# Attention and two MoE layers on one core: the scales of q, k and v from ScalarE's sums of squares in all four batches

## The chip, the cores and the metric

One Trainium2 chip, one of its cores. The metric is device time in microseconds (us) of one launch; the kernel before was run three times, and its median is 1267.02 us (1266.43 to 1269.06).

## What is computed

Four batches of attention (8 heads, 576 rows, head size 64), whose softmax is cut off below the row's maximum minus tau, then two MoE layers over the 2304 rows that come out (512 wide, 2048 hidden), the first with a rational activation, the second with a piecewise quadratic one. Cut to what matters here:

```python
scores = matmul(q, k.T) / sqrt(64)
scores = where(scores >= max(scores) - tau, scores, -1e9)
attn = exp(scores - max(scores)); attn /= sum(attn) + 1e-9
x = matmul(attn, v)                    # (4, 8, 576, 64) -> (2304, 512)
x = rational(x @ moe_w_in) @ moe_w_out
out = quadratic(x @ moe2_w_in) @ moe2_w_out
```

## The kernel before, in words

The work is done batch by batch. A batch's attention turns q, k and v (float32) into pairs of float16 numbers (a high part and the rest), and for that each tensor gets a scale, a power of two. q and k are prepared for two heads at a time (`prep_pair`, lines 316 to 356; four pairs a batch), v once a batch (`prep_v`, lines 289 to 314).

In batches 1 to 3 the scale comes from the largest magnitude. VectorE reduces the loaded float32 tile to one number per partition (line 332 for q and k in one instruction, line 300 for v in two: 2048 columns, then 512). TensorE spreads these numbers over the partitions and VectorE takes the maximum over them (`everywhere`, lines 179 to 189); `power` (lines 155 to 162) makes the power of two and its reciprocal in three small VectorE instructions. Then `split` (lines 205 to 218) writes the high part on ScalarE and the rest on VectorE into the tile `qk` or `v16`, and for q and k a DMA transposes `qk` (line 346). In batch 0, which is prepared before anything else, line 328 gives ScalarE the same task in another way: a Square of the tile, scaled by 2^-32, whose sum over the columns falls out as an extra output; its elementwise result goes into `qk` as waste and is overwritten by the split. `root` (lines 164 to 173) then makes the power of two from the sum of squares, also in three small VectorE instructions. Batch 0's v has a path of its own (`first_v`, lines 484 to 507).

The tiles matter: the loaded q and k have one buffer (`rqk`), `qk` has one, `v16` has one, and the loaded v (`rw`) two. `v16` of the next batch is free once the last product of attention weights and v of the batch before it has been read; line 307 (a GpSimd memset) is the first to write it in the kernel before.

The order of the work is not written out by hand engine by engine. The kernel issues 192 steps (8 phases: MoE 1 and MoE 2 of each batch in turn; a phase has 3 blocks of 192 rows by 8 chunks of the hidden size), and each step makes a first product (line 846), an activation on ScalarE, VectorE and GpSimd (`rational`, lines 719 to 741, in MoE 1; `quadratic`, lines 785 to 794, in MoE 2) and, three steps later, a second product (line 860). Attention of batches 1, 2 and 3 is spread over steps 18 to 50, 60 to 100 and 108 to 147, so that it runs beside the MoE of the batch before. Every unit has a priority by its step, and when the program is built a planner puts the instructions of each engine in one order by priority and by when it reckons them ready. On the chip each engine then works through its own order, and waits where an operand or a buffer is not there. First products go to two PSUM banks in turn.

The line that is replaced, and the one that takes its place in batch 0:

```python
if b == 0:
    for x in range(2):
        A.activation(qk[:, x, :, 0:D], raw[:, x], AF.Square, scale=2.0**-32, accum_out=mx[:, x : x + 1])
    f = small(2, f"qkf{b}_{pr}")
    s = root(f"qkr{b}_{pr}", f, everywhere(f"mqke{b}_{pr}", mx, 2), 2.0**96, n=2)
else:
    V.tensor_reduce(mx, raw.rearrange("p x c d -> p x (c d)"), axis=AX.X, op=ALU.max, apply_absolute_value=True)
    f, s = power(f"qk{b}_{pr}", everywhere(f"mqke{b}_{pr}", mx, 2), 2)
```

Of the kernel before, what the change touches and what calls it, by code (L numbers as in the profile page):

```python
# [9 lines left out]
F16 = mybir.dt.float16  # L10
# [3 lines left out]
AF = mybir.ActivationFunctionType  # L14
ALU = mybir.AluOpType
AX = mybir.AxisListType
# [26 lines left out]
def tile_attention_moe_moe2(  # L43
# [18 lines left out]
    V, A, G, T, Q = nc.vector, nc.scalar, nc.gpsimd, nc.tensor, nc.sync  # L62
    B, H, S, D = q.shape
    P = 128
    NP = H // 2
    NT = S // P
# [17 lines left out]
    ap = ctx.enter_context(tc.tile_pool(name="ap", bufs=2))  # L84
# [23 lines left out]
    def small(n, name, keep=False):  # L108
        if keep:
            return cp.tile([P, n], F32, name=name)  # L110
        tag = "".join(x for x in name if x.isalpha() or x == "_").rstrip("_")
        return sp.tile([P, n], F32, name=name, tag=f"s{n}_{tag}", bufs=4 if tag in ("mx", "nt") else 2)
# [42 lines left out]
    def power(name, src, n, keep=False):  # L155


        f, s = small(n, name + "_f", keep), small(n, name + "_s", keep)
        V.tensor_scalar(f, src, 1.0 / TOP, TINY / TOP, op0=ALU.mult, op1=ALU.max)
        V.tensor_scalar(f.bitcast(I32), f.bitcast(I32), 0x7F800000, None, op0=ALU.bitwise_and)  # L160
        V.reciprocal(s, f)
        return f, s

    def root(name, f, src, up, even=False, n=1):


        s = small(n, name + "_s")
        V.tensor_scalar(f.bitcast(I32), src.bitcast(I32), 1, 0x3F000000 if even else 0x3F800000,
                        op0=ALU.logical_shift_right, op1=ALU.bitwise_and)
        top = TOP / 2 if even else TOP  # L170
        V.tensor_scalar(f, f, up / top, (2.0 if even else 1.0) * TINY / top, op0=ALU.mult, op1=ALU.max)
        V.reciprocal(s, f)
        return s
# [5 lines left out]
    def everywhere(name, src, n, keep=False, place=None):  # L179


        r = small(n, name, keep)
        if place is None:
            place = ps_1.tile([P, 512], F32, name="pm" + name, tag="aux")
        pm = place[:, 0 : n * P].rearrange("p (n q) -> p n q", n=n)
        for i in range(n):
            T.matmul(pm[:, i], src[:, i : i + 1].to_broadcast([P, P]), ident, start=True, stop=True)
        V.tensor_reduce(r, pm, axis=AX.X, op=ALU.max)  # L188
        return r
# [15 lines left out]
    def split(hi, lo, src, scale=None, on_vector=True):  # L205

        if scale is None:
            A.copy(hi, src)  # L208

            n = E // 4 if tuple(src.shape) == (P, E) else None  # L210
            for p in [slice(c, c + n) for c in range(0, E, n)] if n else [slice(None)]:
                G.tensor_tensor(lo[:, p], src[:, p], hi[:, p], op=ALU.subtract)  # L212
        elif on_vector:
            A.activation(hi, src, AF.Copy, scale=scale)
            V.scalar_tensor_tensor(lo, src, scale, hi, op0=ALU.mult, op1=ALU.subtract)
        else:
            A.activation(src, src, AF.Copy, scale=scale)
            split(hi, lo, src)
# [63 lines left out]
    f_x, s_x = [None] * B, [None] * B  # L282
# [3 lines left out]
    def whole(x):  # L286
        return x[..., 0 : NT * P, :].rearrange("h (p t) d -> p h (t d)", t=NT)

    def prep_v(b, on_vector=True):

        raws = []
        mx = small(2, f"mv{b}")
        for g in range(2):
            raw = rp.tile([P, H if g else H * NT, D], F32, name=f"rv{b}_{g}", tag="rw")
            if g:
                for i in range(2):
                    Q.dma_start(raw[i * ST : (i + 1) * ST], v[b, :, NT * P :, :].rearrange("h p d -> p h d"))
            else:
                Q.dma_start(raw.rearrange("p (h t) d -> p h (t d)", h=H), whole(v[b]))
            V.tensor_reduce(mx[:, g : g + 1], raw.rearrange("p t d -> p (t d)"), axis=AX.X, op=ALU.max,  # L300
                            apply_absolute_value=True)
            raws.append(raw)
        m1 = small(1, f"mv1{b}")
        V.tensor_reduce(m1, mx, axis=AX.X, op=ALU.max)
        f_x[b], s_x[b] = power(f"v{b}", everywhere(f"mve{b}", m1, 1), 1, True)
        vv = ap.tile([P, H * (NT + 1), 2 * D + 2], F16, name=f"v16_{b}", tag="v16", bufs=1)
        G.memset(vv[:, :, D : D + 1], 1.0)
        for g, raw in enumerate(raws):
            n = H if g else H * NT
            for n0 in range(0, n, 8):  # L310
                n1 = min(n, n0 + 8)
                to = vv[:, g * H * NT + n0 : g * H * NT + n1]
                split(to[:, :, 0:D], to[:, :, D + 1 : 2 * D + 1], raw[:, n0:n1], s_x[b], on_vector)
        return vv

    def prep_pair(b, pr, on_vector=True):
        raws = rp.tile([P, 2, C + 1, D], F32, name=f"rqk{b}_{pr}", tag="rqk", bufs=1)
        raw = raws[:, :, 0:C, :]
        for x, src in enumerate((q, k)):
            Q.dma_start(raws[:, x].rearrange("p (a c) d -> p a (c d)", a=2)[:, :, 0 : NT * D],  # L320
                        whole(src[b, 2 * pr : 2 * pr + 2]))
            for ab in range(2):
                Q.dma_start(raw[ab * ST : (ab + 1) * ST, x, NT, :], src[b, 2 * pr + ab, NT * P :, :])
        mx = small(2, f"mqk{b}_{pr}")
        qk = ap.tile([P, 2, C, 2 * D], F16, name=f"qk{b}_{pr}", tag="qk", bufs=1)
        if b == 0:
            for x in range(2):
                A.activation(qk[:, x, :, 0:D], raw[:, x], AF.Square, scale=2.0**-32, accum_out=mx[:, x : x + 1])
            f = small(2, f"qkf{b}_{pr}")
            s = root(f"qkr{b}_{pr}", f, everywhere(f"mqke{b}_{pr}", mx, 2), 2.0**96, n=2)  # L330
        else:
            V.tensor_reduce(mx, raw.rearrange("p x c d -> p x (c d)"), axis=AX.X, op=ALU.max, apply_absolute_value=True)
            f, s = power(f"qk{b}_{pr}", everywhere(f"mqke{b}_{pr}", mx, 2), 2)

        con = sp.tile([P, 4], F32, name=f"con{b}_{pr}", tag="con", bufs=3)
        V.scalar_tensor_tensor(con[:, 0:1], f[:, 0:1], cflag, f[:, 1:2], op0=ALU.mult, op1=ALU.mult)
        V.tensor_scalar(con[:, 1:2], con[:, 0:1], -1.0, None, op0=ALU.mult)
        V.scalar_tensor_tensor(con[:, 2:3], s[:, 0:1], tau8, s[:, 1:2], op0=ALU.mult, op1=ALU.mult)
        V.tensor_tensor(con[:, 2:3], con[:, 2:3], tlow, op=ALU.min)
        if b == 0:  # L340
            V.tensor_scalar(con[:, 3:4], con[:, 2:3], STEEP, -LARGEST, op0=ALU.mult, op1=ALU.max)
        for x in range(2):
            split(qk[:, x, :, 0:D], qk[:, x, :, D : 2 * D], raw[:, x], s[:, x : x + 1], on_vector)
        if b > 0 or pr < 2:
            qkT = ap.tile([P, 2 * C, P], F16, name=f"qkT{b}_{pr}", tag="qkT")
            Q.dma_start_transpose(out=qkT, in_=qk.rearrange("p x c d -> p (x c d)"))
            qT, kT = qkT[:, 0:C], qkT[:, C : 2 * C]
            kT2 = ap.tile([P, C, P], F16, name=f"kT2{b}_{pr}", tag="kT2")
        else:
            qT, kT, kT2 = (ap.tile([P, C, P], F16, name=f"{x}{b}_{pr}", tag="eT" if pr == 2 else "hl", bufs=N_ROW)  # L350
                           for x in ("qT", "kT", "kT2"))
            for x, t in enumerate((qT, kT)):
                Q.dma_start_transpose(out=t, in_=qk[:, x].rearrange("p c d -> p (c d)"))
        Q.dma_start(kT2[0:D], kT[D : 2 * D])
        Q.dma_start(kT2[D : 2 * D], kT[0:D])
        return con, qT, kT, kT2
# [515 lines left out]
    for n in range(N_FIRST):  # L872
        with at(36 * n / N_FIRST - 40):
            next(att)
        while halves and len(halves) * N_FIRST > 2 * NCH * (N_FIRST - 1 - n):
            with at(2.4 * (2 * NCH - len(halves)) - 40):
                i, x = halves.pop(0)
# [83 lines left out]
```

## Time and profile before

| | |
|---|---|
| Median of three runs | 1267.02 us (1266.43 to 1269.06) |
| The profiled execution's own time | 1266.28 us |
| Its span | 1264.5 us |
| Mean granted TensorE clock | 0.956 |
| TensorE matmul busy | 1096.8 us (87% of the span) |
| VectorE busy | 1003.2 us (79%) |
| ScalarE busy | 824.5 us (65%) |
| GpSimd busy | 534.4 us (42%) |

The span is the part of the execution between its first and last instruction; the time has 1.8 us more around it. A busy share is a mean over the whole span, and the stages of this kernel are limited by different engines, so the stretches have to be read one by one. In rows of the trace PE is TensorE's matmul, PEld its weight load, DVE is VectorE, ACT ScalarE, POOL GpSimd and SP the queue that issues the DMAs; L332 is line 332 of the kernel.

### The profile page before, as it was taken

What the parts mean: (1) busy time and instruction counts of PE and PEld (TensorE: products, weight loads), DVE (VectorE), ACT (ScalarE), POOL (GpSimd) and SP (SyncE); (2) the same over time, 40 slices, a digit from 0 to 9 for tenths busy, and PEclk for the clock granted to TensorE, in tenths of its full rate; (3) what the DMA queues carried; (4) which work ended last, traced back from release to release, by engine and by line L of the source; (5) the groups of instructions that cost most, each with busy time, mean ns of one, the idle gap of its engine ahead of it and who ended that gap; (6) DMA issues with size and microseconds to landing.
All of it is one profiled execution on the core that took longest, in us unless ns stands there. A gap on an engine that the chain in (4) does not pass through costs nothing.

```text
span 1264.5 us, 31682 instructions
## 1 busy us (share of the span) xinstructions
PE 1096.8 (87%) x12618; PEld 985.3 (78%) x12618; DVE 1003.2 (79%) x2371; ACT 824.5 (65%) x1473; POOL 534.4 (42%) x700
## 2 busy tenths in 40 slices
PE   2788778668788998999799999998889998999998
PEld 1454445567788887899688898997778998999997
DVE  7767977899997877789999766899997767897431
ACT  2476767668686677667676666777765766775332
POOL 3324546576553645421355454313454553222221
PEclk9797898779899999999999999999999999999999
DMA  7656657633427545933398548522784469006000
GB/s 206 221 171 213 231 193 248 239 114 98 117 73 234 114 98 100 241 124 84 73 225 193 94 91 205 178 53 58 214 185 76 102 148 243 14 2 237 32 14 26
DMA packets 220341, 176.40 MB, mean 139 GB/s; under 512 B 182048, under 2 KB 193312, under 8 KB 212000
## 3 DMA queue, kind: packets, MB, share of 16 engines
q1 hardware_dynamic: 220192, 174.36, 51.6%
q8 instruction: 99, 1.62, 0.5%
q14 instruction: 50, 0.41, 0.1%
HBM read 106.83 MB, written 21.50 MB: 101 GB/s over the span
## 4 chain that ended last, share of the span: by engine, by line
PE 37%; DVE 32%; DMA 11%; ACT 8%; issue 5%; POOL 5%; SPq 2%; DVEq 0%; ACTq 0%; POOLq 0%
PE ph L846 14%; PE acc L860 14%; DMA eT<-hl 6%; DVE e L387 3%; DVE sc L425 2%; PE pv L596 2%; DVE t L734 2%; DMA qkT<-qk 2%; PE pv L413 2%; DVE t L740 2%; DVE t L729 2%; DVE wt L229 2%; DMA rqk<-in_k_dram 2%; POOL hl L398 1%; DVE t L730 1%
## 5 line engine op out<-in xcount | busy, mean ns | idle before, releaser
L860 PE MATMUL acc<-gg,wc 128*128 128x192 f16 x4608 | 427.6, 247 | 16.7 <-DVE mye L188 8.4
L846 PEld LDWEIGHTS <-wc 128*128 128x128 f16 x4608 | 389.4, 99 | 30.0 <-DVE t L731 14.7
L860 PEld LDWEIGHTS <-wc 128*128 128x128 f16 x4608 | 383.7, 98 | 19.4 <-issue 17.8
L212 POOL TENSOR_TENSOR gg<-t,gg 128x384 f16<-128x384 f32 x192 | 187.6, 978 | 407.0 <-ACT gg L208 332.4
L846 PE MATMUL ph<-xT,wc 128*128 128x192 f16 x2304 | 220.1, 253 | 19.8 <-DVE t L731 15.3
L846 PE MATMUL ph<-yT,wc 128*128 128x192 f16 x2304 | 216.6, 246 | 2.3 <-DVE t L731 1.9
L398 POOL TENSOR_TENSOR hl<-e,hl 128x256 f16<-128x256 f32 x216 | 154.3, 735 | 0.0
L208 ACT CAST gg<-t 128x384 f16<-128x384 f32 x192 | 97.2, 508 | 83.9 <-DVE t L793 39.4
L387 DVE SCALAR_TENSOR_TENSOR e<-sc,nt,e 128x576 f32<-128x576 f32 x108 | 95.7, 886 | 33.0 <-ACT e L386 32.2
L792 DVE SCALAR_TENSOR_TENSOR t<-t,c 128x384 f32<-128x384 f32 x96 | 63.5, 662 | 72.6 <-ACT t L791 72.5
L386 ACT ACTIVATE e<-sc,nt,con 128x576 f32<-128x576 f32 x108 | 93.5, 866 | 7.2 <-POOL hl L398 0.2
L395 ACT CAST hl<-e 128x576 f16<-128x576 f32 x108 | 72.2, 669 | 35.6 <-DVE e L387 34.7
L727 ACT ACTIVATE t<-ph,sc 128x384 f32<-128x384 f32 x96 | 55.2, 575 | 60.8 <-PE ph L846 60.5
L791 ACT ACTIVATE t<-ph,c 128x384 f32<-128x384 f32 x96 | 64.0, 666 | 47.2 <-PE ph L846 46.7
L396 POOL TENSOR_TENSOR hl<-e,hl 128x64 f16<-128x64 f32 x108 | 40.0, 371 | 126.9 <-ACT hl L395 126.5
L413 PE MATMUL pv<-v,eT 128*128 128x65 f16 (+3 forms) x1680 | 70.7, 194 | 25.2 <-DMA eT<-hl 24.9
L425 DVE TENSOR_SCALAR_CACHE_REDUCE sc<-s 128x576 f32<-128x576 f32 x108 | 80.9, 749 | 13.3 <-PE s L380 12.8
L413 PEld LDWEIGHTS <-eT 128*128 128x128 f16 (+1 forms) x1680 | 62.9, 100 | 35.0 <-DMA eT<-hl 32.4
L732 ACT ACTIVATE t<-t,lc 128x384 f32<-128x384 f32 x96 | 67.9, 707 | 20.4 <-DVE t L729 19.8
L734 DVE SCALAR_TENSOR_TENSOR t<-t,ka,t 128x384 f32<-128x384 f32 x96 | 68.4, 713 | 13.9 <-ACT t L733 13.4
L212 POOL TENSOR_TENSOR wh<-wt,wh 128x256 f16<-128x256 f32 x64 | 60.6, 977 | 41.5 <-ACT wh L208 32.1
L212 POOL TENSOR_TENSOR wc<-wt,wc 128x256 f16<-128x256 f32 x64 | 55.4, 897 | 47.1 <-ACT wc L208 47.1
(233 smaller groups left out, 1901.5 us busy)
## 6 DMA issues: line engine op xcount, KB each, us to landing
wc<-scratch SPq DMA_DIRECT2D x56, 1024.0 KB, 5.9
rw<-in_moe_w_in_dram SPq DMA_DIRECT2D x16, 1024.0 KB, 5.9
rw<-in_moe_w_out_dram SPq DMA_DIRECT2D x16, 1024.0 KB, 5.6
scratch<-wc SPq DMA_DIRECT2D x8, 1024.0 KB, 5.8
scratch<-wh SPq DMA_DIRECT2D x16, 512.0 KB, 3.5
rqk<-in_q_dram SPq DMA_DIRECT2D x16, 256.0 KB, 3.0
rqk<-in_k_dram SPq DMA_DIRECT2D x16, 256.0 KB, 3.1
kT<-qkT SPq DMA_DIRECT2D x28, 144.0 KB, 2.4
```

Of the source, the lines that this page charges most:

```text
L208: A.copy(hi, src)
L212: G.tensor_tensor(lo[:, p], src[:, p], hi[:, p], op=ALU.subtract)
L386: A.activation(e, s, AF.Exp, bias=nb, scale=con[:, 0:1])
L387: V.scalar_tensor_tensor(e, s, th, e, op0=ALU.is_ge, op1=ALU.mult)
L395: A.copy(hi, e)
L398: G.tensor_tensor(lo_w[:, p], e[:, whole][:, p], hi[:, whole][:, p], op=ALU.subtract)
L413: T.matmul(pv[rows, 0:w], eT[:, c, cols], vv[:, h * NT + x if x < NT else H * NT + h, at : at + w], start=(n == 0), stop=(n == len(blocks) ...
L425: V.tensor_scalar(s, banks[:, 0:S], 1.0, -LARGEST, op0=ALU.mult, op1=ALU.max, accum_out=mx)
L732: A.activation(r, u, AF.Ln, bias=lc[:, 1:2], scale=lc[:, 0:1])
L734: V.scalar_tensor_tensor(s, s, ka[:, 0:1], r, op0=ALU.add, op1=ALU.mult)
L846: last = T.matmul(ph[:, f, :], w[:, wx, kt, f * P : (f + 1) * P], rhs, start=(n == 0), stop=(n == 3 * KT - 1))
L860: T.matmul(dst, w[:, wx, f, d * P : (d + 1) * P], gg[:, gx, f, :], start=(i == 0 and f == 0 and n == 0 and d % 2 == 0), stop=(i == NCH - 1 ...
```

## The change

In batches 1 to 3 the two kinds of VectorE reduction go away. For each pair of heads ScalarE makes two Squares with a sum over the columns (576 columns each, q then k), as batch 0 has them; for v it makes two (2048 and 512 columns), whose waste goes into `v16`, so that tile is now allotted ahead of the loads. `root` takes the place of `power` for these scales. Batch 0 and `first_v` stay.

```diff
-    def root(name, f, src, up, even=False, n=1):
+    def root(name, f, src, up, even=False, n=1, keep=False):
...
-        s = small(n, name + "_s")
+        s = small(n, name + "_s", keep)
...
         mx = small(2, f"mv{b}")
+        vv = ap.tile([P, H * (NT + 1), 2 * D + 2], F16, name=f"v16_{b}", tag="v16", bufs=1)
         for g in range(2):
...
-            V.tensor_reduce(mx[:, g : g + 1], raw.rearrange("p t d -> p (t d)"), axis=AX.X, op=ALU.max,
-                            apply_absolute_value=True)
+            n0, n1 = (H * NT, H * (NT + 1)) if g else (0, H * NT)
+            A.activation(vv[:, n0:n1, 0:D], raw, AF.Square, scale=2.0**-32, accum_out=mx[:, g : g + 1])
             raws.append(raw)
         m1 = small(1, f"mv1{b}")
         V.tensor_reduce(m1, mx, axis=AX.X, op=ALU.max)
-        f_x[b], s_x[b] = power(f"v{b}", everywhere(f"mve{b}", m1, 1), 1, True)
-        vv = ap.tile([P, H * (NT + 1), 2 * D + 2], F16, name=f"v16_{b}", tag="v16", bufs=1)
+        f_x[b] = small(1, f"v{b}_f", True)
+        s_x[b] = root(f"v{b}", f_x[b], everywhere(f"mve{b}", m1, 1), 2.0**96, keep=True)
         G.memset(vv[:, :, D : D + 1], 1.0)
...
-        if b == 0:
-            for x in range(2):
-                A.activation(qk[:, x, :, 0:D], raw[:, x], AF.Square, scale=2.0**-32, accum_out=mx[:, x : x + 1])
-            f = small(2, f"qkf{b}_{pr}")
-            s = root(f"qkr{b}_{pr}", f, everywhere(f"mqke{b}_{pr}", mx, 2), 2.0**96, n=2)
-        else:
-            V.tensor_reduce(mx, raw.rearrange("p x c d -> p x (c d)"), axis=AX.X, op=ALU.max, apply_absolute_value=True)
-            f, s = power(f"qk{b}_{pr}", everywhere(f"mqke{b}_{pr}", mx, 2), 2)
+        for x in range(2):
+            A.activation(qk[:, x, :, 0:D], raw[:, x], AF.Square, scale=2.0**-32, accum_out=mx[:, x : x + 1])
+        f = small(2, f"qkf{b}_{pr}")
+        s = root(f"qkr{b}_{pr}", f, everywhere(f"mqke{b}_{pr}", mx, 2), 2.0**96, n=2)
```

## Rows read from the trace of the kernel before

**Rows 1.** The page, part 1: busy us, share of the span, instructions.

```profile
PE 1096.8 (87%) x12618; PEld 985.3 (78%) x12618; DVE 1003.2 (79%) x2371; ACT 824.5 (65%) x1473; POOL 534.4 (42%) x700
```

**Rows 2.** The page, part 4: the chain that ended last, shares of the span by engine.

```profile
PE 37%; DVE 32%; DMA 11%; ACT 8%; issue 5%; POOL 5%; SPq 2%; DVEq 0%; ACTq 0%; POOLq 0%
```

**Rows 3.** Windows, three stretches: length, busy us by engine, clock, DMA share, GB/s.

```profile
300.00:350.00 50.00, 36.50 (x374) 34.02 (x372) 49.90 (x126) 36.68 (x68) 25.89 (x31) 0.86 0.38 98
600.00:675.00 75.00, 64.08 (x781) 58.05 (x780) 74.97 (x195) 54.58 (x102) 36.18 (x47) 0.98 0.71 164
875.00:925.00 50.00, 41.32 (x496) 37.54 (x494) 50.00 (x119) 34.92 (x65) 23.50 (x32) 0.97 0.77 201
```

**Rows 4.** Those three stretches summed: L332 alone, then L300 alone.

```profile
sum 175.00, DVE 5.35; mean DVE 1.78
...
sum 175.00, DVE 5.90; mean DVE 1.97
```

**Rows 5.** Windows 250:300, 575:600 and 825:875 summed: all, L332 alone, L300 alone.

```profile
sum 125.00, PE 107.02 PEld 102.91 DVE 120.10 ACT 92.58 POOL 50.65; mean PE 35.67 PEld 34.30 DVE 40.03 ACT 30.86 POOL 16.88
...
sum 125.00, DVE 2.71; mean DVE 0.90
...
sum 125.00, DVE 2.93; mean DVE 0.98
```

**Rows 6.** Windows of the MoE 1 stretch before attention of batches 2 and 3.

```profile
550.00:575.00 25.00, 25.00 (x301) 24.96 (x299) 21.72 (x39) 18.01 (x34) 5.49 (x6) 1.00 0.12 43
800.00:825.00 25.00, 25.00 (x327) 24.78 (x325) 21.98 (x47) 19.41 (x37) 6.94 (x8) 1.00 0.46 147
```

**Rows 7.** Groups by line, VectorE: busy us, mean ns, idle us before, its releaser.

```profile
L332 DVE TENSOR_REDUCE mqk<-rqk 128x2 f32<-128x1152 f32 x12 | 16.2, 1347 | 7.1 <-DMA rqk<-in_k_dram 7.1
...
L300 DVE TENSOR_REDUCE mv<-rv 128x1 f32<-128x2048 f32 (+1 forms) x6 | 8.8, 1472 | 0.0
```

**Rows 8.** Waits in total: us, times, longest us.

```profile
DVE mqk L332 <- DMA rqk<-in_k_dram: 7.1, 6, 1.9
```

**Rows 9.** Groups by line, VectorE: first small instruction of `power` and of `root`.

```profile
L159 DVE TENSOR_SCALAR qk_f<-mqke 128x2 f32<-128x2 f32 x12 | 4.2, 351 | 0.1
L168 DVE TENSOR_SCALAR qkf<-mqke 128x2 int32<-128x2 int32 x4 | 1.1, 282 | 0.1
```

**Rows 10.** Timeline of ScalarE in batch 0: start us, length us, the Squares of L328.

```profile
9.70 0.68 ACT L328 ACTIVATE qk<-rqk 128x576 f16<-128x576 f32 x1 [2.76 <-DMA rqk<-in_q_dram]
10.29 0.19 ACT L328 ACTIVATION_READ_ACCUMULATOR qk<-rqk 128x1 f32 x1
10.46 0.68 ACT L328 ACTIVATE qk<-rqk 128x576 f16<-128x576 f32 x1
```

**Rows 11.** Groups by line, ScalarE: one kind of instruction at 384 and 576 columns.

```profile
L208 ACT CAST gg<-t 128x384 f16<-128x384 f32 x192 | 97.2, 508 | 83.9 <-DVE t L793 39.4 <-DVE t L740 20.7 <-PE acc L860 17.8
...
L395 ACT CAST hl<-e 128x576 f16<-128x576 f32 x108 | 72.2, 669 | 35.6 <-DVE e L387 34.7
```

**Rows 12.** Timelines of VectorE and PE: two reductions, each followed by its reader on PE.

```profile
305.11 1.34 DVE L332 TENSOR_REDUCE mqk<-rqk 128x2 f32<-128x1152 f32 x1
...
306.59 0.68 PE L187 MATMUL pmmqke<-ident,mqk 128*128 128x128 f32 x4 [1.11 <-DVE rm L700]
...
335.30 1.33 DVE L332 TENSOR_REDUCE mqk<-rqk 128x2 f32<-128x1152 f32 x1
...
405.73 0.64 PE L187 MATMUL pmmqke<-ident,mqk 128*128 128x128 f32 x4
```

**Rows 13.** Timelines of VectorE, POOL and PE: batch 2's v.

```profile
325.27 2.27 DVE L300 TENSOR_REDUCE mv<-rv 128x1 f32<-128x2048 f32 x1
...
541.97 0.28 POOL L307 MEMSET v<- 128x40 f16 x1 [4.65 <-PE pv L413]
...
582.27 0.41 PE L187 MATMUL pmmve<-ident,mv 128*128 128x128 f32 x2
```

**Rows 14.** Timeline of ScalarE: the one load of an activation table.

```profile
0.73 1.28 ACT L92 ACT_TABLE_LOAD   x1 [0.73 <-PEq L946]
```

## The prediction, on record before the changed kernel was run

> **What bounds the kernel now.** I read the page's busy shares first: TensorE is busy 87% of the span, VectorE 79%, ScalarE 65% [rows 1]. None is full, so the means decide nothing. The chain of waits comes next: 37% of it is TensorE's, 32% VectorE's, only 8% ScalarE's [rows 2]; two engines take turns. Windows of 25 and 50 us show where. In 300 to 350, 600 to 675 and 875 to 925, where a batch's preparation and first attention rows run beside MoE 1, VectorE is busy 174.9 of 175 us, while TensorE is busy 141.9 and ScalarE 126.2 [rows 3]: there VectorE alone sets the pace, and TensorE has 33 us to spare. In 250 to 300, 575 to 600 and 825 to 875 VectorE is at 120.1 of 125 (96%) with TensorE at 107.0 [rows 5]: nearly so. In MoE 1 ahead of attention, 550 to 575 and 800 to 825, TensorE is busy 25.0 of 25.0 at a granted clock of 1.00, the full 2.4 GHz [rows 6]; time taken from VectorE there buys nothing.
>
> **What is removed.** Twelve reductions of q and k at 1.347 us, 16.2 us, and six of v, 8.8 us: 25.0 us of VectorE [rows 7]. What they are worth depends on where they stand.
> - In the three full stretches stand 5.35 us of line 332 and 5.90 of line 300, 11.25 us [rows 4]. With VectorE never idle its queue gets shorter by just that, and TensorE's 33 us of slack can take it up: worth 11.25.
> - In the three nearly full stretches stand 2.71 and 2.93, 5.64 us [rows 5]. Between nothing and all of it; VectorE's idle 4.9 us there show that other waits intervene, so I take half: 2.8.
> - The other 25.0 - 16.9 = 8.1 us (six reductions of q and k) stand where VectorE has gaps or TensorE is full. I count them at nothing. What hides them is the wait for the load: VectorE idled 7.1 us in front of six of the twelve [rows 8]. If the cover were gone they would be worth 8.1.
> Removed: 14.05 us, at most 25.0. The low bound comes from the readers. A reduction of pair 1 of a batch is read by its matmul within 6 us (three of them, at 305 the matmul follows at once); the others run far ahead, such as that at 335.30, read at 405.73 [rows 12]. If only the three count, 3 x 1.34 = 4.0 us.
>
> **What is added.** Batch 0's Squares give the price. Square and accumulator read follow each other 0.59 and 0.17 us apart, so one costs ScalarE 0.76 us, although the instruction lasts 0.68 [rows 10]. For q and k 24 x 0.76 = 18.2 us. No row has a Square of 2048 columns, so I scale: a cast takes 508 ns at 384 columns and 669 at 576, 0.84 ns a column [rows 11]; 0.76 + 1472 x 0.00084 = 2.00 us for 2048 and 0.76 - 0.05 = 0.71 for 512, 2.7 a batch, 8.1 in all. ScalarE gets 26.3 us, VectorE loses 25.0; as engine time the trade is even. It pays only if ScalarE has room: it is busy 72% of the full stretches [rows 3].
> - Of ScalarE's busy time, 8% of 1264.5 = 101 us lies on the chain, 12% of 824.5 [rows 1, 2]. At that share the Squares cost 3.2 us. From below: nothing, if all fall into gaps. From above: VectorE's own share, 405 of 1003 us or 40%, 10.6 us.
> - The wait for the raw q and k moves with them. VectorE's 7.1 us [rows 8] become ScalarE's, with the Exp, casts and PSUM reads of attention and MoE queued behind in the same order. At 12%: 0.9 us; from above the whole 7.1; from below nothing.
> - `root` for `power` is three small instructions for three. The first takes 282 ns in place of 351 [rows 9]; over 15 uses that is 1.0 us of VectorE at best. Nothing counted; its cover is that both readings hold stray long ones.
> - A new wait: the Squares write `qk` and `v16`, which have one buffer each, where the reductions wrote neither. For q and k the transposing DMA that frees `qk` is issued ahead of the next pair's load on SP, so the load still comes last; SP's own order does not change. For v it matters: batch 2's reduction ran at 325.27, but `v16` came free only near 541.97, when GpSimd's memset was released, and the number is read at 582.27 [rows 13]. The Squares get 40 us for 2.7, enough; batch 3 has the like. So no latency, but these 5.4 us of ScalarE move to stretches where TensorE is full and ScalarE busy 18.0 and 19.4 of 25 [rows 6]; that is inside the 12%. GpSimd's memset may fall in behind a Square: 0.28 us, covered by the same 40.
> - Squares need no other activation table: a single load, at 0.73 us, served batch 0's Squares and every Exp [rows 14].
>
> **The sum,** against the profiled execution's own 1266.28 us (span 1264.5 and 1.8 around it): 1266.28 - 14.05 + 3.2 + 0.9 = 1256.3. That execution is 0.7 below the median of the three runs, so on the median's footing 1257.0, a gain of 10.0 us.
>
> **A rule that speaks against it.** On the trace, one pass over q and k costs VectorE 1.35 us and ScalarE 2 x 0.76 = 1.52 [rows 7, 10]. The Trainium skill, "ScalarE: Activation LUTs", section "Rules for kernel authors", says to give multiplications and maxima to VectorE and not to ScalarE, since VectorE is up to about three times faster per element in bf16. Here, in float32, the rows make ScalarE only 13% dearer for q and k; for v, 2.7 against 2.9, cheaper by the estimate. By that rule the change would lose, which is the second rival below.
>
> **The rivals.**
> - *The removed time was filler.* The planner places early whatever it reckons ready, so a reduction read 70 us later may have cost nobody anything. Then the gain is the 4.0 us of pair 1, the cost 4.1, the time 1267.1. For it: rows 12. Against it: VectorE without a gap in 175 us, filler or not [rows 3].
> - *ScalarE's queue holds up the others.* A Square of 2 us, or one waiting for its load, stands ahead of the instructions that empty PSUM, and TensorE has two banks for first products. Place: the stretches where TensorE is full, and the attention rows. Price: 40% of 26.3 and all the 7.1 of waiting, 17.7 us, against 14.05: 3.6 us slower, 1270.6. It decides once ScalarE's cost passes 14.05 + 2.5. For it: batches 2 and 3's v lands where TensorE is full [rows 6]. Against it: ScalarE holds only 8% of the chain [rows 2]. This is where the skill's rule would lead.
> - *All of it counts.* The whole 25.0 us leave the path and ScalarE costs 4.1: 1246.1. Against it: the six reductions behind a load wait [rows 8].
>
> A planner works on all this anew, so instructions elsewhere may change places too; no row prices that, and it is why the range reaches past the terms' own.
>
> **How the numbers follow.** 0.2%, about 2.5 us, is what a measurement of this kernel can tell from no change. My forecast has 0.52: the gain between 5 and 15 us, 1252 to 1262. The filler case 0.15, the ScalarE queue 0.25, all of it 0.08. Faster is 0.52 + 0.08 = 0.60, same 0.15, slower 0.25. The range takes in the forecast, the filler case and the nearer half of both outer cases: 1247 to 1271.
>
> **What would show it.** Right: VectorE's busy time falls to about 978 us and ScalarE's rises to about 851; the stretches of full VectorE come out shorter by some 11 us in all and TensorE's share in them rises; v's Squares of batches 2 and 3 stand after the last product of the batch before. Wrong: waits of ScalarE for the load of k beyond some 4 us followed by idle TensorE; TensorE waiting for first-product banks in the stretches of rows 6; or VectorE still full over the same 175 us, filled by other work.

## The result and the profile after

The changed kernel takes 1248.24 us (median of four, 1242.5 to 1254.8) beside 1266.72 for the kernel before (four, 1260.6 to 1269.1): ratio 0.9873, interval [0.9836, 0.9909]. (The recorded ratio is not the quotient of the two medians, which is 0.9854.) By the medians it is 18.5 us faster where 10.0 were forecast, by the interval 11.5 to 20.8: inside the range of 1247 to 1271 but near its low end. Executions of one and the same kernel lie up to 17 us apart here, so single traces are read below for where things stand, and medians for what they cost.

The page of the changed kernel, profiled in an execution of 1242.5 us, the fastest of the four: its span, part 1 and part 4 [rows 1, 2].

```profile
span 1240.7 us, 31727 instructions
...
PE 1091.9 (88%) x12618; PEld 984.5 (79%) x12618; DVE 977.1 (79%) x2353; ACT 842.9 (68%) x1533; POOL 543.0 (44%) x700
...
PE 35%; DVE 19%; DMA 9%; ACT 6%; POOL 6%; issue 6%; SPq 1%; DVEq 0%; ACTq 0%; POOLq 0%
```

VectorE lost 26.1 us of busy time. ScalarE gained 18.4, not 26.3. Since the span also shrank by 23.8, VectorE's busy share stayed at 79%. Its part of the chain reads 19% where the chain before had 32%, but that is no result: the shares printed here sum to 82%, those before to 100%, and a second profile of the changed kernel, in the run that times it again below, has 27% with all of the chain printed:

```profile
PE 39%; DVE 27%; DMA 12%; POOL 8%; issue 8%; ACT 6%; SPq 1%; DVEq 0%; ACTq 0%; POOLq 0%
```

The windows that answer to [rows 3], where VectorE is full in the changed kernel, with their sum.

```profile
300.00:325.00 25.00, 17.28 (x176) 15.43 (x174) 25.00 (x67) 20.91 (x43) 13.16 (x17) 0.93 0.29 86
575.00:650.00 75.00, 66.06 (x815) 61.36 (x813) 74.97 (x194) 57.45 (x110) 37.84 (x46) 0.98 0.70 176
825.00:900.00 75.00, 65.82 (x785) 61.45 (x784) 75.00 (x197) 59.00 (x114) 29.38 (x36) 0.98 0.58 140
sum 175.00, PE 149.16 PEld 138.24 DVE 174.97 ACT 137.36 POOL 80.38; mean PE 49.72 PEld 46.08 DVE 58.32 ACT 45.79 POOL 26.79
```

In windows of 25 us VectorE is still full for 175 us. The stretches lie elsewhere: the first has lost its second half, the second comes 25 us earlier, the third 50 us earlier and 25 us longer. TensorE gets 149.2 us of work done in them in place of 141.9. ScalarE is busy 137.4 us there in place of 126.2, and is still not full. Windows this wide cannot show a change of 11 us; with 5 us ones, from 200 to 1000 us, those in which VectorE is busy 4.98 us or more add up to 275 us before and 245 in the changed kernel (255 in its second profile).

The windows that answer to [rows 6], MoE 1 ahead of attention.

```profile
525.00:550.00 25.00, 25.00 (x303) 24.97 (x302) 21.09 (x39) 20.41 (x40) 5.06 (x6) 1.00 0.29 102
775.00:825.00 50.00, 50.00 (x631) 49.56 (x630) 44.76 (x97) 39.81 (x76) 12.07 (x16) 1.00 0.39 104
```

TensorE is as full as before, at a granted clock of 1.00, with three of the four Squares of batches 2's and 3's v now beside it; the fourth starts at 523.10, just ahead of the first window.

The groups of the Squares on ScalarE, all 32 of q and k (8 of them batch 0's) and the six of v, which stand in the place of [rows 7].

```profile
L328 ACT ACTIVATE qk<-rqk 128x576 f16<-128x576 f32 x32 | 21.7, 677 | 26.8 <-DMA rqk<-in_q_dram 15.9 <-DMA rqk<-in_k_dram 5.6 <-DMA qkT<-qk 3.8
...
L302 ACT ACTIVATE v<-rv 128x2048 f16<-128x2048 f32 (+1 forms) x6 | 7.6, 1270 | 1.8 <-DMA rv<-in_v_dram 1.4 <-PE pv L410 0.4
```

And their waits in total [rows 8].

```profile
ACT qk L328 <- DMA rqk<-in_q_dram: 15.9, 4, 9.8
...
ACT qk L328 <- DMA rqk<-in_k_dram: 5.6, 6, 1.6
ACT qk L328 <- DMA qkT<-qk: 3.8, 2, 2.2
...
ACT qk L328 <- issue: 1.4, 1, 1.4
```

Batch 0's eight alone waited 13.5 us of this for q and 2.3 for k (the same view from 0 to 95 us). So the new Squares wait 2.4 + 3.3 us for their loads, where VectorE had waited 7.1, and 3.8 us, in two waits together, for the transposing DMA that frees `qk`.

The timeline of ScalarE at batch 2's v [rows 13] (start, duration, what it is, and the wait ahead of it).

```profile
523.10 1.91 ACT L302 ACTIVATE v<-rv 128x2048 f16<-128x2048 f32 x1 [0.42 <-PE pv L410]
524.92 0.18 ACT L302 ACTIVATION_READ_ACCUMULATOR v<-rv 128x1 f32 x1
525.01 0.61 ACT L302 ACTIVATE v<-rv 128x512 f16<-128x512 f32 x1
```

The same view at a pair of q and k [rows 10].

```profile
399.05 0.68 ACT L328 ACTIVATE qk<-rqk 128x576 f16<-128x576 f32 x1 [1.60 <-DMA qkT<-qk]
399.63 0.19 ACT L328 ACTIVATION_READ_ACCUMULATOR qk<-rqk 128x1 f32 x1
399.73 0.67 ACT L328 ACTIVATE qk<-rqk 128x576 f16<-128x576 f32 x1
```

v's Square starts as soon as the last product of batch 1's attention releases `v16`, as foreseen, and lasts 1.91 us. The pair at 399.05 is the only new one that runs back to back, 0.68 us apart. But whatever ScalarE does next after a new Square of q or k starts 0.66 to 0.69 us after it in 23 of 24 cases, although an accumulator read of 0.19 us stands between: the read hides in the overlap of neighbours.

### The profile page after: what moved, and what is told of

It reads as the page before. It is cut to its first block, busy times and chain, and to the rows that moved or that the text cites. A ratio compares the mean times of both kernels' runs of the same rounds, so it can differ in the third digit from the quotient of the medians.

```text
span 1240.7 us, 31727 instructions
## 1 busy us (share of the span) xinstructions
PE 1091.9 (88%) x12618; PEld 984.5 (79%) x12618; DVE 977.1 (79%) x2353; ACT 842.9 (68%) x1533; POOL 543.0 (44%) x700
## 4 chain that ended last, share of the span: by engine, by line
PE 35%; DVE 19%; DMA 9%; ACT 6%; POOL 6%; issue 6%; SPq 1%; DVEq 0%; ACTq 0%; POOLq 0%
PE ph L843 15%; PE acc L857 15%; DMA eT<-hl 7%; POOL hl L395 3%; DVE e L384 2%; PE pv L410 2%; DVE t L731 2%; DVE t L726 2%; DVE sc L422 2%; DVE t L737 1%; DMA qkT<-qk 1%; DVE t L728 1%; POOL gg L212 1%; DVE t L727 1%; ACT hl L392 1%
## 5 line engine op out<-in xcount | busy, mean ns | idle before, releaser
L843 PEld LDWEIGHTS <-wc 128*128 128x128 f16 x4608 | 389.8, 99 | 37.4 <-issue 20.8
L212 POOL TENSOR_TENSOR gg<-t,gg 128x384 f16<-128x384 f32 x192 | 193.3, 1008 | 380.0 <-ACT gg L208 330.0
L393 POOL TENSOR_TENSOR hl<-e,hl 128x64 f16<-128x64 f32 x108 | 43.3, 401 | 145.0 <-ACT hl L392 141.4
L422 DVE TENSOR_SCALAR_CACHE_REDUCE sc<-s 128x576 f32<-128x576 f32 x108 | 80.9, 749 | 13.5 <-PE s L377 12.7
L731 DVE SCALAR_TENSOR_TENSOR t<-t,ka,t 128x384 f32<-128x384 f32 x96 | 70.1, 730 | 11.1 <-ACT t L730 10.8
```

Of the source, the lines that this page charges most:

```text
L422: V.tensor_scalar(s, banks[:, 0:S], 1.0, -LARGEST, op0=ALU.mult, op1=ALU.max, accum_out=mx)
L731: V.scalar_tensor_tensor(s, s, ka[:, 0:1], r, op0=ALU.add, op1=ALU.mult)
L843: last = T.matmul(ph[:, f, :], w[:, wx, kt, f * P : (f + 1) * P], rhs, start=(n == 0), stop=(n == 3 * KT - 1))
```

## The experiments

The kernel's order of instructions is made by a planner when the program is built. Taking 18 instructions from one engine and giving 30 to another changes the order as well. So there are two theories: **1**, VectorE's time is what counts; **2**, the other order is. Several runs keep the order exactly: the planner sees the full instruction, and its columns are cut or doubled in the finished program.

**Before's order, all 18 reductions short.**

```diff
+            CUT.append(V.tensor_reduce(mx, raw.rearrange("p x c d -> p x (c d)"), axis=AX.X, op=ALU.max, apply_absolute_value=True).ins.name)
...
+    def short(args):
+        return [replace(args[0], ap=[*args[0].ap[:-1], (1, 8)]), *args[1:]]
+    for block in nc.main_func.blocks:
+        for at, ins in enumerate(block.instructions):
+            if ins.name in CUT:
+                block.instructions[at] = replace(ins, ins=short(ins.ins))
```

> The kernel before with its order of instructions on every engine kept exactly, and only the 18 reductions made short once the order is fixed (8 columns for each number in place of 512 to 2048; the scales then come from fewer columns, which is the work left out). VectorE loses about 22 of its 25 us of reductions; ScalarE gets nothing. Theory 1 (VectorE's time in the stretches where it is full is what counts): about 12 us faster than before, near 1254, shorter stretches of full VectorE, nothing gained before 275 us. Theory 2 (the changed kernel gains because the planner made another order): 0 to 4 us faster, 1263 or more.

Measured: 1253.03 us beside 1264.50, ratio 0.9913 [0.9886, 0.9940], 11.5 us faster. The groups of its reductions, and its windows at the times of [rows 3].

```profile
L332 DVE TENSOR_REDUCE mqk<-rqk 128x2 f32<-128x16 f32 x12 | 2.0, 164 | 6.3 <-DMA rqk<-in_k_dram 6.2
...
L300 DVE TENSOR_REDUCE mv<-rv 128x1 f32<-128x8 f32 x6 | 0.9, 153 | 1.5 <-DMA rv<-in_v_dram 1.4
```

```profile
300.00:350.00 50.00, 38.42 (x408) 36.10 (x406) 48.41 (x127) 38.85 (x72) 27.66 (x32) 0.90 0.34 88
600.00:675.00 75.00, 64.56 (x807) 58.86 (x807) 74.23 (x197) 54.86 (x105) 38.27 (x51) 0.98 0.84 192
875.00:925.00 50.00, 44.21 (x570) 39.92 (x569) 49.83 (x124) 36.54 (x69) 27.19 (x37) 1.00 0.80 216
```

22.1 us of VectorE went (25.0 - 2.9), with no other order and nothing given to ScalarE, and 11.5 us of time went with them, 0.52 us for each. At the old times VectorE now has gaps of 1.6, 0.8 and 0.2 us, and TensorE does 147.2 us in place of 141.9. Theory 1 holds for the size.

**The same, only pairs 1 and 2 and v short; and only pairs 0 and 3 short.** In the diff of the first run the condition is added in these two forms:

```diff
+            CUT.extend([...] * (pr in (1, 2)))
...
+            CUT.extend([...] * (pr in (0, 3)))
```

> The order of the kernel before, kept exactly; of the 18 reductions only those that stood in full or nearly full stretches of VectorE are made short (pairs 1 and 2 of each batch, and v: 16.9 us of reductions). Theory 1: these carry the whole gain of the run with all 18 short, so 10 to 13 us below the kernel before. If the place in the trace says nothing: 16.9/25 of that gain, 7 to 8 us.

> The counterpart: only the six reductions of pairs 0 and 3 are made short, 8.1 us that stood where VectorE has gaps or TensorE is full. Theory 1: nothing, within 2 us of the kernel before. If the place says nothing: 3 to 4 us faster.

Measured: 1257.08 beside 1264.04 (0.9952 [0.9932, 0.9973]), 7.0 us faster; and 1261.66 (0.9980 [0.9962, 0.9998]), 2.4 us faster. The first took away 15.0 us of reductions (16.9 became 1.9), the second 7.1 (8.1 became 1.0), so 0.46 and 0.33 us for each. The first run misses what theory 1 expected, 10 to 13 us. These are the numbers expected if the place says nothing. The spans of the two profiled executions say the opposite:

```profile
span 1253.4 us, 31682 instructions
```

```profile
span 1264.4 us, 31682 instructions
```

Beside the 1264.5 of the trace before that is 11.1 and 0.1 us, theory 1 to the letter. But the twelve executions of each kernel spread over 17 and 12 us, and one execution cannot outweigh them. The place of the reductions is not shown to matter as much as the prediction had it; the two parts together, 9.4 us, agree with the first run.

**The changed kernel's order, Squares short (one column in 64), and Squares long.**

```diff
+            CUT.extend([A.activation(...).ins.name] * (b > 0))
...
+                block.instructions[at] = replace(ins, ins=short(ins.ins), outs=short(ins.outs))
```

In the long form only q's and k's Squares change: each group of 64 columns is read twice, so 576 columns become 1152.

```diff
+                block.instructions[at] = replace(ins, ins=long(ins.ins, lambda d: [d[0], (64, 9), (0, 2), (1, 64)]), outs=long(ins.outs, lambda d: [*d[:-1], (1, 128)]))
```

> The changed kernel with its order kept exactly, and the 30 Squares of batches 1 to 3 made short once the order is fixed (one column in 64; the scales come from fewer columns, which is the work left out). ScalarE loses about 18 of the 26 us that the Squares cost it. If ScalarE's time costs 12%, as the prediction has it: 2 to 3 us faster than the changed kernel. If it costs 40% (the second rival): about 7 us faster. If it costs nothing: the same within 2 us.

> The changed kernel with its order kept exactly, and the 24 Squares of q and k in batches 1 to 3 made twice as long once the order is fixed (each reads its 576 columns twice and fills the whole of its part of the tile, which the split overwrites anyway). ScalarE gets about 11.5 us more. At the predicted 12% that is 1 to 2 us slower than the changed kernel; at 40%, the second rival, 4 to 5 us slower.

Measured: 1246.45 for the short ones (0.9859 [0.9821, 0.9897]) and 1249.43 for the long ones (0.9868 [0.9839, 0.9897]). The changed kernel timed again beside the long ones gave 1247.39, its first timing 1248.24. The Squares' groups, short and then long:

```profile
L328 ACT ACTIVATE qk<-rqk 128x9 f16<-128x9 f32 (+1 forms) x32 | 11.1, 347 | 32.0 <-DMA rqk<-in_q_dram 20.0 <-DMA rqk<-in_k_dram 8.8 <-DMA qkT<-qk 2.0
...
L302 ACT ACTIVATE v<-rv 128x32 f16<-128x32 f32 (+1 forms) x6 | 1.5, 289 | 3.1 <-DMA rv<-in_v_dram 1.6 <-PE pv L410 1.5
```

```profile
L328 ACT ACTIVATE qk<-rqk 128x1152 f16<-128x1152 f32 (+1 forms) x32 | 33.2, 1036 | 25.2 <-DMA rqk<-in_q_dram 18.5 <-DMA rqk<-in_k_dram 4.2 <-DMA qkT<-qk 1.4
```

ScalarE's busy time went from 842.9 to 826.3 us in the one and from 843.5 to 853.4 in the other. 16.6 us less brought 1 to 2 us, 9.9 more cost 2. The intervals overlap with the changed kernel's, so each run alone settles little. Set against each other, the two differ by 27.1 us of ScalarE and by 3.0 us of time (by the ratios 1.1), with some 6 us of uncertainty by the two intervals. That excludes 40%, which would be 10.8 us, and fits 12% as well as no price at all. The waits for q's and k's loads do not go when the Squares shrink: 20.0 and 8.8 us with short ones, 15.9 and 5.6 in the changed kernel.

**Squares and reductions together.** The reductions are put back beside the Squares, their result unused, first with one column in 64, then in the same order at full length.

```diff
+            CUT.append(V.tensor_reduce(old, raw[..., 0], axis=AX.X, op=ALU.max, apply_absolute_value=True).ins.name)
```

> The changed kernel with the old reductions put back beside the Squares, their result unused, and made short (one column in 64). The planner makes a new order for it. Theory 1: the time of the changed kernel within the spread that another order brings, so 1242 to 1258. Theory 2 gives no number: any order may come out.

> The same order to the instruction as the run with the short reductions put back, but the 18 reductions have their full length again: VectorE has its 25 us back, ScalarE keeps its 26 us of Squares. Theory 1: 10 to 14 us slower than the run with the short ones. Theory 2: 0 to 4 us slower, since the order is the same.

Measured: 1256.78 (0.9954 [0.9935, 0.9974]) and 1269.24 (1.0041 [1.0027, 1.0054]). The groups of the reductions in the two:

```profile
L334 DVE TENSOR_REDUCE oqk<-rqk 128x2 f32<-128x18 f32 x12 | 2.1, 175 | 8.9 <-DMA rqk<-in_k_dram 8.9
L306 DVE TENSOR_REDUCE ov<-rv 128x1 f32<-128x32 f32 x3 | 0.6, 194 | 0.0
L306 DVE TENSOR_REDUCE ov<-rv 128x1 f32<-128x8 f32 x3 | 0.5, 158 | 0.7 <-DMA rv<-in_v_dram 0.7
```

```profile
L334 DVE TENSOR_REDUCE oqk<-rqk 128x2 f32<-128x1152 f32 x12 | 16.1, 1346 | 8.1 <-DMA rqk<-in_k_dram 8.0
...
L306 DVE TENSOR_REDUCE ov<-rv 128x1 f32<-128x2048 f32 x3 | 6.8, 2276 | 0.0
L306 DVE TENSOR_REDUCE ov<-rv 128x1 f32<-128x512 f32 x3 | 2.0, 673 | 0.0
```

21.7 us of VectorE cost 12.5 us at the same order, 0.57 us for each: the first run's price again, in a third order, with ScalarE's Squares present. With both kinds of work the kernel is in this order slower than the kernel before, so Squares alone do not make it faster. The short form is 9 us slower than the changed kernel, though it adds only 3.2 us of VectorE. It has another order; but with the reductions VectorE's waits for loads came back as well, 8.9 + 0.7 us, and this run does not separate the two.

**The same work in another order.** One number of the priorities is moved, in the kernel before and in the changed one.

```diff
-                with at(t - 1.5):
+                with at(t - 1.4):
                     next(atts[u[1]])
```

> The kernel before with the same work, and only the priority of the attention units moved by a tenth of a step (1.4 in place of 1.5 steps ahead), so that the planner makes another order. Theory 1: within 3 us of before. Theory 2 (orders differ by as much as the change brought): it may lie 5 to 15 us off, either way.

> The changed kernel with the same tenth of a step. Theory 1: it stays 8 to 16 us below the kernel before with the same tenth of a step. Theory 2: the difference between those two may be anything from 0 to 30 us, and this kernel may lie 5 to 15 us off the changed one.

> The kernel before with the priority of the attention units moved a tenth of a step the other way (1.6 steps ahead). The tenth of a step late gave 6 to 8 us more with the same work, so this should differ from before by a like amount, in either direction: 1257 to 1272.

> The changed kernel with the same tenth of a step early. If the work (VectorE's time less ScalarE's cost) is worth about 10 us and an order a few us either way, it lies 5 to 16 us below the kernel before with the same tenth; a difference outside that would say that the order decides more than the work.

> The changed kernel unchanged, timed again beside the kernel before on the chip of the other runs of this call, since its first four executions spread over 12 us. If theory 1 and a good order each gave their part: 13 to 17 us below the kernel before. If the first four were lucky: 9 to 12 us.

| order | kernel before | changed kernel | difference |
|---|---|---|---|
| as it is | 1265.37 | 1247.39 (0.9860 [0.9829, 0.9890]) | -18.0 |
| a tenth of a step late | 1270.78 (1.0061 [1.0032, 1.0089]) | 1256.18 (0.9943 [0.9922, 0.9965]) | -14.6 |
| a tenth early | 1269.10 (1.0037 [1.0019, 1.0054]) | 1259.53 (0.9951 [0.9928, 0.9974]) | -9.6 |

The ratios are to the kernel before, as it is: 1264.50 beside the late pair, 1265.37 in the other rows. With no change of work an order moves the time by 4 to 12 us. Both kernels have the best of their three orders as they are. In each of the three the changed one wins, by 14.1 us in the mean. The changed kernel timed again, 18.0 us below, is past even the 13 to 17 expected of it: its first four executions were not lucky ones.

Where the order shows first: the windows from 0 to 275 us, TensorE's first products alone (busy us and count in brackets), of the kernel before, the kernel before with short reductions, the kernel before replanned late, the changed kernel, its second profile, the changed kernel replanned late, and Squares together with short and with full reductions.

```profile
0.00:275.00 275.00, 18.19 (x153) 0.85 0.64 210
```

```profile
0.00:275.00 275.00, 19.25 (x166) 0.86 0.66 210
```

```profile
0.00:275.00 275.00, 18.46 (x153) 0.85 0.65 210
```

```profile
0.00:275.00 275.00, 22.93 (x206) 0.87 0.64 210
```

```profile
0.00:275.00 275.00, 22.08 (x192) 0.86 0.63 206
```

```profile
0.00:275.00 275.00, 21.96 (x200) 0.86 0.64 210
```

```profile
0.00:275.00 275.00, 21.78 (x197) 0.87 0.65 211
```

```profile
0.00:275.00 275.00, 19.56 (x168) 0.89 0.66 211
```

A step has 24 first products. The orders made without the reductions are some two steps further in MoE 1 at 275 us; shorter reductions in the old order bring half a step. But the last two rows have one and the same order: full reductions take back 29 of its products, more than a step. So the lead is not the order's alone. It comes in a stretch where the prediction counted almost nothing; how much of it is the order's, and why the planner comes to it there, was not found out.

## Why the prediction was right, and where not

- **VectorE is what the removed work is worth: right, in size.** 14.05 us was the forecast for 25.0 us of reductions; at 0.52 to 0.57 us for each, the runs give 13.0 to 14.4. The first rival, filler that costs nobody anything, falls: 4.0 us was its gain, 11.5 was measured with nothing but the reductions shortened. The third rival, "all of it counts", comes nearer to the measured time (1246.1) than the forecast does (1257.0), and the gain is past the 5 to 15 us that the forecast allowed; but its mechanism falls too, since about half of the reductions counted and not the whole. The time lies in the range because the range took in the nearer half of that rival and reached past the terms for a new order; so there is luck in the number.
- **The split by stretches: not shown.** 11.25 + 2.8 us in the full and nearly full stretches and nothing in the gaps became 7.0 and 2.4 by the medians. The cover named for the gaps was misread: the six reductions that wait for their load are not the six counted at nothing. Two of them, at 590.43 and 851.11, stand in nearly full stretches, and those at 109.73 and 717.23 waited for nothing. The rule "full VectorE counts whole, the rest not at all" gave a good sum, perhaps from two errors that cancel.
- **ScalarE's cost: right in kind, its work mis-sized.** 26.3 us was the estimate of its work; the busy time rose by 18.4. A pitch of 0.76 us was taken from batch 0's first pair, which is the odd one; the new Squares hold up what follows by 0.66 to 0.69 us, those of v by 1.91 and 0.61 where 2.00 and 0.71 were scaled from two casts. That makes 23.9 us; the other 5.5 between it and 18.4 was not traced. Its price, 12%, fits the runs but is not told apart from nothing. The Trainium skill, "ScalarE: Activation LUTs", section "What ACT_TABLE_LOAD costs", has 186 ns + 0.833 ns a column for an ACTIVATE with immediate scale and bias, 1.89 us for 2048 columns by estimate; the trace agrees, with 1.91.
- **The second rival, ScalarE's queue, did not come.** TensorE stayed full in MoE 1, and the 40% that it needed is excluded by the short and long Squares. The Trainium skill, "ScalarE: Activation LUTs", section "Rules for kernel authors", gives multiplications and maxima to VectorE, which would have led to this rival; the measurement goes the other way here, where VectorE was the engine without room.
- **The new wait on `qk`: wrong for two Squares.** "So the load still comes last" does not hold for two, which waited 3.8 us for the transposing DMA. For v the slack was there: the Squares of batch 2 end at 525.6 and the number is read at 563.9, those of batch 3 at 789.6 and 822.4.
- **The sign "stretches of full VectorE come out shorter": not settled.** The prediction named a VectorE still full over the same 175 us as a sign against it, and in windows of 25 us that came, with more TensorE work in them. In windows of 5 us the full time is shorter in all three orders: 275 to 245, late 270 to 220, early 300 to 265; 275 to 250 with the order held and the reductions short. But the changed order with short Squares has 285, so one trace can be off by more than the 11 us foretold.
- **The term that failed:** "instructions elsewhere may change places too; no row prices that". It stood at nothing in the sum. Work alone gives -13.0 to -14.4 for VectorE and, at 0 to 0.2 us for each of 18.4, 0 to +4 for ScalarE: -9 to -14, beside the 10.0 of the forecast. The measured change is 18.0 to 18.5 us. The 4 to 9 us between are argued to be the order; no run holds the old order and does the new work, so this is a remainder and not a measurement. That an order alone moves the time by as much is measured. A second cause was not tested: VectorE's 7.1 us of waits for k's load left its queue with the reductions, while the runs that only shorten them keep such waits there (6.3 us in the first). The prediction charged ScalarE for them and credited VectorE with nothing. At the 0.33 to 0.57 us that work was worth they would be 2 to 4 us by estimate. How the remainder divides between the two stays open.

## What to carry to other kernels

Read the windows for an engine that is full, and price work taken from it by a run that keeps the order of instructions and only shortens the work; here that came within 3 us of the forecast made from the windows. Where a planner orders the program, a change of work is also a new order: time the same work in two or three neighbouring orders on both sides before a difference of a per cent is put down to the change. An engine that stays full in wide windows is no sign of failure if another engine gets more done beside it. And work moved to another engine takes its waits along, which shortened work does not show.

## What was not expected of the hardware

Eighteen reductions cost about half their length and not all or none of it, in two orders (0.52 and 0.57 us for each us; 0.46 and 0.33 in two parts of the trace). On ScalarE the next instruction starts 0.66 to 0.69 us after a Square of 576 columns although an accumulator read of 0.19 us stands between, so the sum costs little there, and 29.6 us of added instruction time (Squares and reads: 16.3 and 7.6, 4.5 and 1.2) raised the busy time by 18.4. Executions of the same program spread by 3 to 17 us, mostly about 1%, which is why the 0.2% that the prediction took for a measurement's limit was too fine.
